# Chunked attention feeding a routed expert layer: SP's flag read and the early group's place moved

## The chip, the cores and the metric

The kernel runs on one core of a Trainium2 chip. A core has TensorE (PE: products, and PEld: the loads of their weights), VectorE (DVE), ScalarE (ACT), GpSimd (POOL) and SyncE (SP, which only issues DMAs here). Every engine takes its instructions strictly in program order and waits on semaphores. The metric is the time of one execution in device microseconds; lower is better.

## The reference

```python
def _attn_ref(q, k, v):                  # q, k, v: 8 x 8 x 576 x 64
    ...
    scores = scale * np.matmul(q_c, k_c.transpose(0, 1, 2, 4, 3))   # within chunks of 64
    scores = scores - np.max(scores, axis=-1, keepdims=True)
    attn = np.exp(scores)
    attn = attn / (np.sum(attn, axis=-1, keepdims=True) + 1e-09)
    out = np.matmul(attn, v_c)
...
def _moe_ref(x, w_gate, w1, w2, capacity):   # x: 4608 x 512, E = 8, F = 1024, capacity 80
    logits = x @ w_gate
    expert_idx = np.argmax(logits, axis=1)
    ...
    gate_w = probs[np.arange(N), expert_idx]
    out = np.zeros((N, D), dtype=np.float32)
    for e in range(E):
        tok_idx = np.where(expert_idx == e)[0]
        ...
        if len(tok_idx) > capacity:      # the 80 tokens of the largest gate weight stay
            gw = gate_w[tok_idx]
            tok_idx = tok_idx[np.argpartition(-gw, capacity)[:capacity]]
        h = np.maximum(x[tok_idx] @ w1[e], 0.0)
        out[tok_idx] = gate_w[tok_idx, None] * (h @ w2[e])
```

The attention's output, as 4608 rows of 512, is the expert layer's x. Rows that no expert keeps are zero.

## The kernel before

**Attention.** 18 pairs of row tiles (36 tiles of 128 rows) run through a pipeline written out by hand: scores, row maxima, exponential, values, division (`divide`), a transpose for the gate (`xtrans`), gate products (`gate_mm`). SP loads q, k, v and stores the rows to a scratch tensor `xs` (`store`). Eight groups of four tiles hold rows 0 to 511 of the eight batches, the ninth (`T == 8`) the last 64 rows of all of them, the "tail". In passing, SP also loads the weights of experts 0 and 1 in 512 KB pieces (`early_pieces`).

**Routing.** For each tile the gate's chain (maximum, exponential, winner, gate weight as a level) runs over DVE, ACT and POOL. Counting products (`tally`) find each expert's threshold; then every kept token gets a place, one-hot matrices (`hot`) and 36 products sum the candidates (`cand`), ranks follow, and `place` yields the row numbers of six groups of 128 expert rows (`gi`), gate weights and targets. `keep_warm(n)` issues n products whose result nobody reads. A flag (`flag_i`) says whether a general path has to run behind the program.

**The early group.** Up to 64 tokens each of experts 0 and 1 from the first 28 tiles are chosen ahead (`spec_...`): two one-hot products for each tile (one for each expert), a sum into row numbers `gi0`, and a gather of 128 rows into `x0`. `spec_units` queues its two layers as 19 units (transposes `turned`, eight `l1`, eight `l2`), and `fill(k)` puts the next k of them on TensorE between steps of the routing. Its buffers `xT0`, `hs0` and `ht0` take turns in the ring of buffers named xT.

**Expert stage.** `experts` takes groups 1 to 5: a gather by POOL (`rows`, tiles xgc), a transpose (xpc), layer 1 in two halves (hc), a transpose (hpc), layer 2 (yc), a multiplication by the gate weight and a scatter to `out`. `LATER` is the order in which SP issues the loads of experts 2 to 7 (`part`: 2 MB each, w1 and w2 apart) and the zeroing of `out` (`clear`: 1 MB each) around these groups. Group 1 needs experts 0 to 2, group 2 experts 2 and 3, group 3 experts 4 and 5, group 4 5 and 6, group 5 6 and 7. The expert stage's memory lies over that of the attention's buffers, so a load also waits for the last reader of what lay there.

## Time and profile before

| | us |
|---|---|
| median of 3 runs | 255.55 (255.5 to 257.46) |
| the profiled execution, its own time | 257.42 |
| its span, first to last instruction | 255.6 |
| PE busy | 226.1 (88%) |
| DVE busy | 118.6 (46%) |
| ACT busy | 67.7 (27%) |
| POOL busy | 57.1 (22%) |

Busy shares are means over stages with different limits, so a stage is read by its windows, its timeline and its waits. Two lines of the page cut the span into 40 slices of 6.39 us each; the one on the DMA engines gives their busy share in tenths:

```
DMA  7999999999999999999400599999999999997211
```

### The profile page before, as it was taken

What the parts mean: (1) busy time and instruction counts of PE and PEld (TensorE: products, weight loads), DVE (VectorE), ACT (ScalarE), POOL (GpSimd) and SP (SyncE); (2) the same over time, 40 slices, a digit from 0 to 9 for tenths busy, and PEclk for the clock granted to TensorE, in tenths of its full rate; (3) what the DMA queues carried; (4) which work ended last, traced back from release to release, by engine and by line L of the source; (5) the groups of instructions that cost most, each with busy time, mean ns of one, the idle gap of its engine ahead of it and who ended that gap; (6) DMA issues with size and microseconds to landing.
All of it is one profiled execution on the core that took longest, in us unless ns stands there. A gap on an engine that the chain in (4) does not pass through costs nothing.

```text
span 255.6 us, 7393 instructions
## 1 busy us (share of the span) xinstructions
PE 226.1 (88%) x3211; PEld 142.1 (56%) x3211; DVE 118.6 (46%) x269; ACT 67.7 (27%) x119; POOL 57.1 (22%) x158
## 2 busy tenths in 40 slices
PE   8699999999999999999999924999809999999980
PEld 5598897888898898888663301233202424232420
DVE  7767696868696878884747210012100211111210
ACT  2214343635363635544051100111000202010000
POOL 9202202222222222385730043000000000000711
PEclk9999999999999999999599995799956999999996
DMA  7999999999999999999400599999999999997211
GB/s 248 393 404 380 383 410 408 407 403 401 393 374 365 408 349 332 374 411 401 164 0 3 171 374 398 398 399 390 407 410 410 406 391 400 398 404 278 106 74 38
DMA packets 34742, 84.73 MB, mean 332 GB/s; under 512 B 3022, under 2 KB 3150, under 8 KB 34704
## 3 DMA queue, kind: packets, MB, share of 16 engines
q1 hardware_dynamic: 33744, 81.31, 83.5%
q0 software_dynamic: 960, 2.88, 3.0%
q8 instruction: 27, 0.44, 0.7%
q14 instruction: 11, 0.09, 0.1%
HBM read 64.00 MB, written 20.45 MB: 330 GB/s over the span
## 4 chain that ended last, share of the span: by engine, by line
PE 69%; SPq 12%; DMA 10%; issue 3%; DVE 2%; ACT 1%; POOL 0%; POOLq 0%; ACTq 0%
PE o L436 14%; PE s L379 12%; PE yc L246 9%; PE hc L213 9%; SPq L1144 8%; DMA w<-in_w 7%; PE px L408 4%; SPq L807 4%; PE pt L408 4%; PE small L491 4%; DMA qb<-in_qk 3%; PE hpc L231 2%; PE hw L776 2%; PE pwarm L776 1%; PE xw L746 1%
## 5 line engine op out<-in xcount | busy, mean ns | idle before, releaser
L213 PE MATMUL hc<-w,xtc 128*32 128x512 f32 x288 | 35.9, 630 | 7.5 <-DMA w<-in_w 7.5
L436 PE MATMUL o<-vb,pT 128*64 128x130 f32 x576 | 36.2, 276 | 0.5 <-ACT pT L417 0.5
L379 PE MATMUL s<-qb 128*64 128x128 f32 x512 | 31.9, 276 | 2.6 <-DMA qb<-in_qk 2.0
L436 PEld LDWEIGHTS o<-vb,pT 128*64 128x64 f32 x576 | 31.7, 135 | 1.7 <-ACT pT L417 0.6
L379 PEld LDWEIGHTS s<-qb 128*64 128x64 f32 x512 | 27.9, 137 | 5.0 <-issue 3.6
L390 DVE TENSOR_REDUCE mx<-s 128x16 f32<-128x1024 f32 x18 | 22.0, 1225 | 14.1 <-PE s L379 13.2
L246 PE MATMUL yc<-w,htc 128*32 128x512 f32 x256 | 28.2, 593 | 0.0
L417 ACT ACTIVATE pT<-pt 128x1024 f32<-128x1024 f32 x18 | 18.3, 1025 | 30.5 <-PE pt L408 28.9
L213 PEld LDWEIGHTS hc<-w,xtc 128*32 128x32 f32 x288 | 9.3, 115 | 29.8 <-issue 21.4
L482 ACT COPY xT<-px 128x1024 f32<-128x1024 f32 x17 | 17.1, 1009 | 23.2 <-PE px L408 23.2
L451 DVE TENSOR_TENSOR x<-o,rc 128x1024 f32<-128x1024 f32 (+1 forms) x20 | 22.4, 1118 | 0.7
L395 DVE TENSOR_TENSOR sm<-s,mx 128x1024 f32<-128x1024 f32 x18 | 22.1, 1228 | 0.6
L265 POOL DMA_INDIRECT out<-x,to x1 | 1.0, 1046 | 81.3 <-SPq L1160 81.3
L246 PEld LDWEIGHTS yc<-w,htc 128*32 128x32 f32 x256 | 8.2, 110 | 18.7 <-issue 18.7
L220 DVE TENSOR_SCALAR hsc<-hc 128x512 f32<-128x512 f32 x5 | 3.5, 692 | 32.1 <-PE hc L213 32.1
L218 ACT ACTIVATE hsc<-hc 128x512 f32<-128x512 f32 x4 | 2.4, 598 | 57.3 <-PE hc L213 57.3
L235 DVE COPY htc<-hpc 128x512 f32<-128x512 f32 x5 | 3.5, 692 | 29.2 <-PE hpc L231 29.2
L592 ACT ACTIVATE lv<-io_b,bo 128x256 bf16<-128x256 bf16 x29 | 12.5, 497 | 3.9 <-DVE bo L572 2.6
L251 DVE TENSOR_SCALAR ysc<-yc,gatec 128x512 f32<-128x512 f32 x4 | 3.0, 750 | 21.2 <-PE yc L246 21.2
L408 PE MATMUL px<-ct,x 64*128 64x64 f32 x272 | 12.4, 229 | 0.5 <-issue 0.5
L408 PE MATMUL pt<-ct,sm 64*128 64x64 f32 x288 | 12.8, 229 | 0.0
L408 PEld LDWEIGHTS pt<-ct,sm 64*128 64x128 f32 x288 | 10.3, 139 | 2.9 <-issue 2.8
(208 smaller groups left out, 268.0 us busy)
## 6 DMA issues: line engine op xcount, KB each, us to landing
w<-in_w SPq DMA_DIRECT2D x12, 2048.0 KB, 20.8
qb<-in_qk SPq DMA_DIRECT2D x32, 512.0 KB, 7.6
vb<-in_vv SPq DMA_DIRECT2D x36, 260.0 KB, 6.8
out<-zero SPq DMA_DIRECT2D x9, 1024.0 KB, 15.4
xs<-x SPq DMA_DIRECT2D x16, 512.0 KB, 7.2
w<-in_w SPq DMA_DIRECT2D x16, 512.0 KB, 7.9
w<-in_qk SPq DMA_DIRECT2D x4, 512.0 KB, 5.2
xs<-x SPq DMA_DIRECT2D x4, 256.0 KB, 8.4
```

Source lines behind the costliest of these rows:

```text
L213: nc.tensor.matmul(h[o:o + 32, :], lhsT=xT[r][:, b, o:o + 32], rhs=getw(groups[r][g])[0][:, b, 512 * f:512 * f + 512], start=(b == 0), sto ...
L246: nc.tensor.matmul(y[o:o + 32, :], lhsT=hT[r][c // 4][:, c % 4, o:o + 32], rhs=getw(groups[r][g])[1][:, c, :], start=(c == 0), stop=(c == ...
L379: nc.tensor.matmul(ps[64 * u:64 * u + 64, t, P * pr:P * pr + P].rearrange("p (h k) -> p h k", h=2), lhsT=t8[:, 1, pr, u, :], rhs=t8[:, 0:3 ...
L390: nc.vector.tensor_reduce(d['mx'], d['s8'], axis=AX.X, op=ALU.max)
L395: nc.vector.tensor_tensor(d['sm'].rearrange("p c k h -> p h c k"), d['s8'], d['mx'][:, :, :, None].to_broadcast([P, 2, 8, 64]), op=ALU.sub ...
L408: nc.tensor.transpose(at[:, 64 * c:64 * c + 64], src(c)[rows], ident[rows, rows])
L417: nc.scalar.activation(d['pT'], pt, AF.Exp, scale=0.125)
L436: nc.tensor.matmul(po[64 * u:64 * u + 64, o:o + 130].rearrange("p (h x) -> p h x", h=2), lhsT=d['pT'][:, u, c:c + 64], rhs=v[:, :, pr, u, ...
L451: nc.vector.tensor_tensor(TT[T][:, r:r + nt, :].rearrange("p r (k h e) -> p (r k) h e", k=4, h=2), pov[..., 0:64], rc[:, :, :, None].to_br ...
L482: nc.scalar.copy(XT[n].rearrange("p c u j -> p u c j"), pm.rearrange("p u (c j) -> p u c j", j=64))
L592: nc.scalar.activation(lv, io_b, AF.Sign, bias=bo[:, rt:rt + 1], scale=-1.0)
L1144: nc.sync.dma_start(w[l], src[e].rearrange("(c p) f -> p c f", p=P))
```

## The change

1. The flag is read by SP behind all loads of the expert stage, no longer ahead of them (`general`, read inside the hand-written part).
2. The early group's `hs0` and `ht0` move into the ring place of `qb2`, and `xT0` into that of `pT`; the one-hot matrices of `hot` leave `qb2` for the places of `x` and `pT`. So other weights lie over them, and the gathers' buffers no longer do.
3. `LATER` puts both first clears ahead of w1 of expert 4, and w2 of expert 4 behind w1 of expert 5.
4. The tail becomes tile group 0 and is stored first; the early group's rows then all lie in the first 3456 rows of `xs`, and tile 3 (rows behind that bound) is left out of it.
5. One product for each early tile yields both experts' row numbers in two columns; the gather becomes two of 64 rows. The products and the gather move ahead of the last tile's gate.
6. Steps of the levels 24 to 27 move from POOL to ACT (`signs`), the count of own tokens covers 28 tiles and moves back, 22 of the 24 keep-warm products behind `spec_gather` go, and the early group's units begin five steps earlier.

```diff
 LG = NT - 1
 HOT = 12
 OB = 171
-LATER = [[(2, 1), (3, 0), (3, 1), (4, 0), (4, 1), (0, 2), (1, 2)], [(5, 0), (6, 0)], [(7, 0), (2, 2), (5, 1), (6, 1)],
-         [(3, 2), (7, 1)] + [(n, 2) for n in range(4, NT)], [], [], []]
+LATER = [[(2, 1), (3, 0), (3, 1), (0, 2), (1, 2), (4, 0)], [(5, 0), (4, 1), (6, 0)],
+         [(7, 0), (2, 2), (5, 1), (6, 1)], [(3, 2), (7, 1)] + [(n, 2) for n in range(4, NT)], [], [], []]
 SPEC = 28
 S0 = 64
+SHOT = ((0, 10), (10, 9), (19, 9))
 
 EARLY = {8: [0], 11: [1], 14: [2], 15: [3, 4], 16: [5, 6, 7, 8], 17: [9, 10, 11], 18: [12], 19: [13, 14], 20: [15]}
 
...
 
-    def rows(t, at):
+    def rows(t, at, n=NT * 512):
 
         return nc.gpsimd.indirect_dma_start(
-            out=t, out_offset=None, in_=xs[:, :],
+            out=t, out_offset=None, in_=xs[0:n, :],
             in_offset=bass.IndirectOffsetOnAxis(ap=at, axis=0),
-            bounds_check=NT * 512 - 1, oob_is_err=False)
+            bounds_check=n - 1, oob_is_err=False)
 
     def experts(pool, pp, gi, si, gate, getw, tag, extra=None, ys0=None):
         groups = [[(4 * r + g) // 3 for g in range(4)] for r in range(NR)]
...
             T, r = divmod(2 * n + 1, 4)
-            if T == 8:
+            if T == 0:
                 for u in range(2):
-                    i = nc.sync.dma_start(
+                    nc.sync.dma_start(
                         xs.rearrange("(b s) d -> s b d", s=576)[
                             512:576, 2 * r - 2 + u:2 * r + 2:2, :],
                         TT[T][64 * u:64 * u + 64, r - 1:r + 1, :])
-                    tc.add_to_no_dep_group("first", i.ins)
             else:
-                i = nc.sync.dma_start(
-                    xs[T * 576:T * 576 + 512].rearrange("(c p) d -> p c d", p=P)[:, r - 1:r + 1],
+                nc.sync.dma_start(
+                    xs[T * 576 - 576:T * 576 - 64].rearrange("(c p) d -> p c d", p=P)[:, r - 1:r + 1],
                     TT[T][:, r - 1:r + 1])
-                if 4 * T >= SPEC:
-                    tc.add_to_no_dep_group("first", i.ins)
 
         def xtrans(n, tag="tp"):
             T, r = divmod(2 * n, 4)
...
                 if 'hot' not in S:
-                    S['hot'] = wk.tile([P, 3, P, HOT], BF16, name="pk", tag="qb2", bufs=1), deque(range(3))
-                oh = S['hot'][0][:, S['hot'][1].popleft()]
+                    pk = wk.tile([P, 2, P, HOT], BF16, name="pk", tag="x")
+                    pl = wk.tile([P, P, HOT], BF16, name="pl", tag="pT")
+                    S['hot'] = deque((pk[:, 0], pk[:, 1], pl))
+                oh = S['hot'].popleft()
                 nc.vector.tensor_tensor(
                     oh[:, :, 0:n], S['io_h'][:, :, 0:n],
                     S['ptok_b'][:, None, rt:rt + n].to_broadcast([P, P, n]), op=ALU.is_equal)
...
+            thr0 = S['thr0'] = gk.tile([P, 2], BF16, name="thr0", tag="thr0", bufs=1)
             with nc.allow_low_precision(reason="whole numbers up to 256"):
                 nc.vector.tensor_scalar(thr0, pn0, 1.0, None, op0=ALU.max)
+
+        def spec_mask():
+            thr0 = S['thr0']
             m0 = S['m0'] = gk.tile([P, 2, SPEC], BF16, name="m0", tag="m0", bufs=1)
             nc.vector.tensor_tensor(m0, kb[:, 0:2, 0:SPEC],
                                     thr0[:, :, None].to_broadcast([P, 2, SPEC]), op=ALU.is_ge)
+            nc.vector.memset(m0[:, :, 3:4], 0.0)
             inc0 = S['inc0'] = gk.tile([P, 2, SPEC], BF16, name="inc0", tag="inc0", bufs=1)
...
 
+        def spec_own():
+            cnt = S['cnt'] = gk.tile([P, NE], BF16, name="cnt", tag="cnt", bufs=1)
+            with nc.allow_low_precision(reason="whole numbers up to 28"):
+                nc.vector.tensor_reduce(cnt, mine[:, 0:SPEC, :].rearrange("p r e -> p e r"),
+                                        axis=AX.X, op=ALU.add)
+
...
             oh = S['oh0', r0]
-            cand0 = S['warm'][0]
+            if 'cand0' not in S:
+                S['cand0'] = ps1.tile([P, 2, 512], F32, name="xw0", tag="tp")[:, 0]
+            cand0 = S['cand0'][0:S0, 0:12].rearrange("p (k e) -> p k e", e=2)
             k = 2 * S.setdefault('chunk0', 0)
             S['chunk0'] += 1
             for j in range(n):
                 rt = r0 + j
-                for e in range(2):
-                    nc.tensor.matmul(
-                        cand0[S0 * e:S0 * e + S0, k:k + 2], lhsT=oh[:, :, j], rhs=comp[:, rt, 0:2, e],
-                        start=j == 0, stop=j == n - 1, tile_position=(0, S0 * e))
+                nc.tensor.matmul(
+                    cand0[:, k:k + 2, :],
+                    lhsT=oh[:, :, j], rhs=comp[:, rt, 0:2, 0:2], start=j == 0, stop=j == n - 1)
 
         def spec_gather():
-            gi0 = mp.tile([P, 1], I32, name="gi0")
+            gi0 = mp.tile([P, 2], I32, name="gi0")
             with nc.allow_low_precision(reason="row numbers are whole and far below 2^24"):
-                nc.vector.tensor_reduce(gi0, S['warm'][0][:, 0:6], axis=AX.X, op=ALU.add)
+                nc.vector.tensor_reduce(
+                    gi0[0:S0], S['cand0'][0:S0, 0:12].rearrange("p (k e) -> p e k", e=2),
+                    axis=AX.X, op=ALU.add)
             x0 = S['x0'] = mp.tile([P, DM], F32, name="x0")
-            apart(rows(x0, gi0), "first")
+            for e in range(2):
+                rows(x0[S0 * e:S0 * e + S0], gi0[0:S0, e:e + 1], 6 * 576)
 
         units = deque()
 
         def spec_units():
-            xT = wk.tile([P, 4, P], F32, name="xT0", tag="xT", bufs=3)
-            hs = wk.tile([P, FF], F32, name="hs0", tag="xT", bufs=3)
-            hT2 = wk.tile([P, 2, 4, P], F32, name="ht0", tag="xT", bufs=3)
-            hT = [hT2[:, f] for f in range(2)]
+            xT = wk.tile([P, 2, 512], F32, name="xT0", tag="pT")[:, 0].rearrange("p (b k) -> p b k", k=P)
+            big = wk.tile([P, 2, FF], F32, name="hs0", tag="qb2", bufs=1)
+            hs = big[:, 0]
+            hT = [big[:, 1, 512 * f:512 * f + 512].rearrange("p (b k) -> p b k", k=P)
+                  for f in range(2)]
             A, B, C = S['warm']
             A4 = A.rearrange("p (b k) -> p b k", k=P)
 
...
             left_add(20)
-            for j in range(24, 28):
-                steps_(nc.gpsimd, j)
+            spec_pos()
             values(35, "s")
-            spec_pos()
+            spec_slot()
+            for r0, n in SHOT:
+                spec_hot(r0, n)
+            xtrans(16)
             gate_mm(7)
             gate_copy(7)
+            for j in range(24, 28):
+                signs(j)
+            for r0, n in SHOT:
+                spec_cand(r0, n)
             divide(34)
-            xtrans(16)
+            spec_gather()
             divide(35)
             store(17)
             early_pieces(20)
-            spec_slot()
             gate_sum(7, gates)
             pops(2)
-            spec_hot(0, 10)
+            spec_own()
             xtrans(17, ("o", "s"))
             gate_mm(8)
-            spec_hot(10, 9)
             flush(gates)
             gate_copy(8)
+            rest(28, "level", "sum")
             psx.close()
             ps1 = psx.enter_context(tc.tile_pool(name="ps2", bufs=1, space=PSUM, reuse_waits="tile"))
             small = S['small'] = ps1.tile([P, 2, 256], F32, name="small2", tag="g")
             two = ps1.tile([P, 2, 512], F32, name="two", tag="s")
             S['warm'] = [ps1.tile([P, 512], F32, name=("xw", "hw", "pwarm")[j], tag=f"o{j}") for j in range(3)]
-            spec_hot(19, 9)
+            spec_units()
             signs(28)
             signs(29)
             gate_sum(8, gates)
             tally(24, 4)
-            spec_cand(0, 10)
-            spec_cand(10, 9)
-            spec_cand(19, 9)
+            fill(1)
             pops(2)
             signs(30)
             signs(31)
             left_add(24)
-            spec_gather()
             flush(gates)
+            rest(32, "sum")
             signs(32)
             for j in range(33, 36):
                 steps_(nc.vector, j)
+            fill(1)
             tally(28, 4)
             left_add(28)
             spec_keep()
-            keep_warm(7)
+            fill(1)
             tally(32, 4)
-            rest(28, "level", "sum")
-            rest(32, "sum")
+            fill(1)
+            threshold()
             rest(32, "inverse", "key")
-            keep_warm(4)
-            threshold()
-            spec_units()
-            keep_warm(6)
+            fill(1)
             mask = gk.tile([P, NE, RT], BF16, name="mask", tag="mask", bufs=1)
             nc.vector.tensor_tensor(
                 mask, kb,
...
             for i, (a, b) in enumerate(((tr_b, mask), (idp, mask), (ones_b, inc))):
                 nc.tensor.matmul(pos.rearrange(fl), lhsT=a, rhs=b.rearrange(fl),
                                  start=i == 0, stop=i == 2)
-            fill(1)
-            keep_warm(5)
-            fill(1)
+            fill(2)
             ptok = S['ptok'] = gk.tile([P, RT], F32, name="ptok", tag="ptok", bufs=1)
             ptok_b = S['ptok_b'] = gk.tile([P, RT], BF16, name="ptok_b", tag="ptok_b", bufs=1)
             with nc.allow_low_precision(reason="whole numbers up to 256"):
...
 
+            homes = {}
             part(2, 0)
             experts(ep, pp, lambda r: (places[0][1][:, r:r + 1] if r < 2 else
                                        places[1][1][:, r - 2:r - 1]),
                     si, gate, weights.get, "c", ahead, S['x0'])
-
-
-    with tc.If(nc.values_load(flag_i[0:1, 0:1], min_val=0, max_val=1) > 0):
+            general = nc.values_load(flag_i[0:1, 0:1], min_val=0, max_val=1)
+
+
+    with tc.If(general > 0):
         with ExitStack() as gctx:
             gp = gctx.enter_context(tc.tile_pool(name="gen", bufs=1))
             lo = gp.tile([P, NE], F32, name="glo")
...
     p = i[:, None]
-    row = np.where(rt < 32, rt // 4 * 576 + rt % 4 * 128 + p,
-                   (2 * (rt - 32) + p // 64) * 576 + 512 + p % 64)
+    row = np.where(rt >= 4, (rt // 4 - 1) * 576 + rt % 4 * 128 + p,
+                   (2 * rt + p // 64) * 576 + 512 + p % 64)
     c[:, C_A:C_A + RT] = row // 64 * 64
     c[:, C_B:C_B + RT] = row % 64
     c[:, C_W8:C_W8 + NE] = NE - np.arange(NE)
...
     t = a[:, :, 512:].reshape(b, h // 2, 2, 64, d).transpose(1, 2, 0, 3, 4)[None]
-    return np.concatenate([m, t], 0).reshape(NT, h // 2, 2, 4, 2, 64, d)
+    return np.concatenate([t, m], 0).reshape(NT, h // 2, 2, 4, 2, 64, d)
 
```

What the order of the built program shows. SP first: before, at the end of the attention (w2_1 is the last early piece, xs the scratch rows, w1_2 to w2_4 the loads of experts 2 to 4, out_0 a clear):

```order
L818 DMA w2_1_1956<-in_w2 128x2x512
L1160 TENSOR_LOAD flag_i_86
L1160 ISA x2
L1144 DMA w1_2_2821<-in_w1 128x4x1024
L1144 DMA w2_2_2823<-in_w2 128x8x512
L1144 DMA w1_3_2825<-in_w1 128x4x1024
L1144 DMA w2_3_2827<-in_w2 128x8x512
L1144 DMA w1_4_2829<-in_w1 128x4x1024
L1144 DMA w2_4_2831<-in_w2 128x8x512
L807 DMA out_0<-zero_75 512x1x512 x2
```

The same place now:

```order
L827 DMA w2_1_1958<-in_w2 128x2x512
L1155 DMA w1_2_2776<-in_w1 128x4x1024
L1155 DMA w2_2_2778<-in_w2 128x8x512
L1155 DMA w1_3_2780<-in_w1 128x4x1024
L1155 DMA w2_3_2782<-in_w2 128x8x512
L816 DMA out_0<-zero_75 512x1x512 x2
L1155 DMA w1_4_2786<-in_w1 128x4x1024
L1155 DMA w1_5_2861<-in_w1 128x4x1024
L1155 DMA w2_4_2863<-in_w2 128x8x512
L1155 DMA w1_6_2865<-in_w1 128x4x1024
L1155 DMA w1_7_2958<-in_w1 128x4x1024
```

and the flag's read, further on:

```order
L1155 DMA w2_6_2963<-in_w2 128x8x512
L816 DMA out_0<-zero_75 512x1x512
L1155 DMA w2_7_3059<-in_w2 128x8x512
L816 DMA out_0<-zero_75 512x1x512 x5
L1170 TENSOR_LOAD flag_i_86
L1170 ISA x2
L1173 COMPARE_AND_BRANCH
```

The read has moved behind the last load and the last clears; two clears stand ahead of w1_4, and w2_4 behind w1_5.

ACT, in the gate of the last tile (lv are level masks of the tiles, ex32 the exponential of the last tile, xT0 the copy of the early group's transposed rows). Before:

```order
L592 ACTIVATE lv28_2353<-io_b_66,bo_79 128x256
L592 ACTIVATE lv29_2355<-io_b_66,bo_79 128x256
L529 ACTIVATE ex32_2359<-sh32_2358 128x32
L592 ACTIVATE lv30_2437<-io_b_66,bo_79 128x256
L592 ACTIVATE lv31_2439<-io_b_66,bo_79 128x256
L592 ACTIVATE lv32_2456<-io_b_66,bo_79 128x256
L770 COPY xT0_2524<-xw_2349 128x512
```

Now:

```order
L590 ACTIVATE lv28_2396<-io_b_66,bo_79 128x256
L590 ACTIVATE lv29_2398<-io_b_66,bo_79 128x256
L779 COPY xT0_2394<-xw_2391 128x512
L527 ACTIVATE ex32_2402<-sh32_2401 128x32
L590 ACTIVATE lv30_2429<-io_b_66,bo_79 128x256
L590 ACTIVATE lv31_2431<-io_b_66,bo_79 128x256
L590 ACTIVATE lv32_2443<-io_b_66,bo_79 128x256
L789 ACTIVATE hs0_2395<-hw_2392 128x512
```

The copy xT0 stood behind all level masks and now stands ahead of the last tile's exponential; the first activation of the early group's layer 1 (hs0) has moved ahead of the routing's ptok.

DVE, from the division of tile 34 (rc34, x8) to the copy of the last transposed tile (xT17; pm0, ptc and pk0 are the early group's places and one-hot matrices, gi0 its row numbers). Before:

```order
L449 TENSOR_SCALAR rc34_2244<-o34_2173 128x8
L450 RECIPROCAL rc34_2244<-rc34_2244 128x8
L451 TENSOR_TENSOR x8_2131<-o34_2173,rc34_2244 128x512
L449 TENSOR_SCALAR rc35_2267<-o35_2214 128x8
L450 RECIPROCAL rc35_2267<-rc35_2267 128x8
L451 TENSOR_TENSOR x8_2131<-o35_2214,rc35_2267 128x512
L718 TENSOR_TENSOR pm0_2274<-small_99,m0_2192 128x56
L720 TENSOR_TENSOR ptc_2275<-pm0_2274 128x28
L561 TENSOR_REDUCE gm28_2283<-small_99 128x4
L528 TENSOR_TENSOR sh28_2279<-small_99,gm28_2283 128x32
L733 TENSOR_TENSOR pk0_2293<-io_h_430,ptc_2275 128x640
L478 COPY xT17_2313<-px17s_2296 128x512
```

Now, from the second and third one-hot group on (pm0, ptc and the first group stand ahead of these rows):

```order
L737 TENSOR_TENSOR pk0_2222<-io_h_432,ptc_2219 128x64x9 x2
L450 TENSOR_SCALAR rc34_2300<-o34_2175 128x8
L451 RECIPROCAL rc34_2300<-rc34_2300 128x8
L452 TENSOR_TENSOR x8_2131<-o34_2175,rc34_2300 128x512
L758 TENSOR_REDUCE gi0_2304<-xw0_2271 64x2
L450 TENSOR_SCALAR rc35_2313<-o35_2209 128x8
L451 RECIPROCAL rc35_2313<-rc35_2313 128x8
L452 TENSOR_TENSOR x8_2131<-o35_2209,rc35_2313 128x512
L559 TENSOR_REDUCE gm28_2324<-small_99 128x4
L526 TENSOR_TENSOR sh28_2320<-small_99,gm28_2324 128x32
L724 TENSOR_REDUCE cnt_2334<-mine_78 128x8
L476 COPY xT17_2354<-px17s_2337 128x512
```

The one-hot groups stand ahead of both divisions, the sum gi0 between them, and the count cnt ahead of the copy.

## Rows read from the trace of the kernel before

**Rows 1.** Waits of SP, which issues the loads: us, times, longest us.

```profile
SPq L1160 <- DVE flag_i L1117: 22.8, 1, 22.8
```

**Rows 2.** Timeline of SP: start us, us, engine, line, operation, out<-in, count.

```profile
117.77 0.86 SPq L818 DMA_DIRECT2D w<-in_w  x1
142.31 21.83 SPq L1144 DMA_DIRECT2D w<-in_w  x6
```

**Rows 3.** Windows: stretch, us, PE PEld DVE ACT POOL, granted clock, DMA share, GB/s.

```profile
124.00:130.00 6.00, 5.58 (x42) 3.63 (x41) 4.91 (x13) 1.37 (x5) 3.52 (x11) 0.64 0.16 51
130.00:136.00 6.00, 6.00 (x76) 3.58 (x76) 2.69 (x15) 2.22 (x9) 1.46 (x2) 1.00 0.01 3
158.00:165.00 7.00, 6.82 (x44) 1.90 (x48) 0.00 (x0) 1.05 (x3) 0.00 (x0) 0.68 1.02 399
165.00:183.00 18.00, 18.00 (x172) 6.15 (x167) 2.08 (x3) 1.89 (x4) 0.00 (x0) 1.00 1.04 396
```

**Rows 4.** Timeline of the expert stage, idle time before and its releaser in brackets.

```profile
149.28 1.10 POOL L177 DMA_INDIRECT xgc<-xs,gic  x1 [17.82 <-PE hw L785]
...
156.39 1.12 PE L202 MATMUL xpc<-ct,xgc 128*128 128x128 f32 x4 [7.92 <-DMA xgc<-xs,gic]
...
158.19 5.74 PE L213 MATMUL hfirst<-w,xtc 128*32 128x512 f32 x32 [0.68 <-ACT xtc L203]
...
191.78 6.00 PE L213 MATMUL hc<-w,xtc 128*32 128x512 f32 x26 [7.51 <-DMA w<-in_w]
```

**Rows 5.** Chain that ended last, by time: start us, us, engine, tile, line.

```profile
124.64 0.87 PE pwarm L669 x4
...
127.64 0.85 PE xw L769 x4
...
129.21 1.06 PE hw L776 x8
130.27 2.09 PE two L1027 x36
...
199.23 3.57 PE hc L213 x32
202.80 6.87 PE yc L246 x64
...
213.10 1.02 PE hpc L231 x8
214.13 0.44 PE xpc L202 x4
```

**Rows 6.** Timeline of the routing.

```profile
113.18 0.69 DVE L451 TENSOR_TENSOR x<-o,rc 128x512 f32<-128x512 f32 x1
...
115.04 0.48 DVE L733 TENSOR_TENSOR pk<-io_h,ptc 128x640 bf16<-128x640 bf16 x1
...
121.57 0.17 DVE L753 TENSOR_REDUCE gi<-xw 128x1 int32<-128x6 f32 x1 [2.78 <-PE xw L746]
...
122.03 1.30 POOL L177 DMA_INDIRECT x<-xs,gi  x1 [3.15 <-DMA xs<-x]
...
123.00 0.29 DVE L572 TENSOR_SCALAR bo<-bb 128x4 f32<-128x4 bf16 x1
...
128.57 0.59 ACT L770 COPY xT<-xw 128x512 f32<-128x512 f32 x1 [4.67 <-PE xw L769]
...
137.55 0.16 DVE L156 TENSOR_REDUCE gic<-small 128x2 int32<-128x4 f32 x1 [1.02 <-PE small L152]
```

**Rows 7.** DMA issues: KB each where known, median us from issue to landing.

```profile
w<-in_w SPq DMA_DIRECT2D x12, 2048.0 KB, 20.8
...
xgc<-xs,gic POOLq DMA_INDIRECT x5, 7.1
...
x<-xs,gi POOLq DMA_INDIRECT x1, 4.0
```

**Rows 8.** Timeline of the end.

```profile
247.99 0.75 DVE L251 TENSOR_SCALAR ysc<-yc,gatec 128x512 f32<-128x512 f32 x1 [6.12 <-PE yc L246]
```

More of the change, by code (lines that the diff above doesn't have):

```diff
@@ L93, in apart @@
         tc.declare_no_dep(
-            inst.ins, group=group, reason="rows of their own",
+            inst.ins, group=group, reason="every store writes rows of its own",
             query=mybir.DependencyQuery(
@@ L617, in tally @@
             U['ph', rt] = ph
-        def own_counts():
-            cnt = S['cnt'] = gk.tile([P, NE], BF16, name="cnt", tag="cnt", bufs=1)
-            with nc.allow_low_precision(reason="whole numbers up to 24"):
-                nc.vector.tensor_reduce(cnt, mine[:, 0:24, :].rearrange("p r e -> p e r"),
-                                        axis=AX.X, op=ALU.add)
         def left_add(rt):
@@ L694, in spec_level, with spec_threshold @@
                 nc.tensor.matmul(pn0, lhsT=ones_b, rhs=S['ge0'][:, b, :], start=b == 0, stop=b == 1)
-        def spec_mask():
-            thr0 = gk.tile([P, 2], BF16, name="thr0", tag="thr0", bufs=1)
+        def spec_threshold():
+            thr0 = S['thr0'] = gk.tile([P, 2], BF16, name="thr0", tag="thr0", bufs=1)
             with nc.allow_low_precision(reason="whole numbers up to 256"):
                 nc.vector.tensor_scalar(thr0, pn0, 1.0, None, op0=ALU.max)
+        def spec_mask():
+            thr0 = S['thr0']
             m0 = S['m0'] = gk.tile([P, 2, SPEC], BF16, name="m0", tag="m0", bufs=1)
@@ L925, in attention_moe @@
                     spec_count()
-                if n == NPAIR - 2:
-                    own_counts()
                 if n < NPAIR - 2:
@@ L936, in attention_moe @@
             xtrans(15)
+            spec_threshold()
             divide(32)
@@ L1134, in attention_moe, with home, part @@
                                                  reuse_waits="tile"))
-            def part(e, l, after=None):
-                w = weights.setdefault(e, [None, None])
-                pool = wp if e in (5, 6) else wp2
-                a, src, n = ((4, w1, FF), (8, w2, DM))[l]
-                w[l] = pool.tile([P, a, n], F32, name=f"w{l + 1}_{e}", tag=f"w{l + 1}")
-                if after is not None:
-                    nc.vector.tensor_copy(w[l][:, 0, 0:1], after)
-                nc.sync.dma_start(w[l], src[e].rearrange("(c p) f -> p c f", p=P))
+            def home(e, l):
+                pool = wp if e in (5, 6) else wp2
+                a, n = ((4, FF), (8, DM))[l]
+                return pool.tile([P, a, n], F32, name=f"w{l + 1}_{e}", tag=f"w{l + 1}")
+            def part(e, l):
+                w = weights.setdefault(e, [None, None])
+                w[l] = homes.pop((e, l), None)
+                if w[l] is None:
+                    w[l] = home(e, l)
+                nc.sync.dma_start(w[l], (w1, w2)[l][e].rearrange("(c p) f -> p c f", p=P))
             def ahead(r):
```

## The prediction, made before the changed kernel was run

> **What bounds the kernel now.** I begin with the waits of SP, since that queue issues every load. It stands 22.8 us at one instruction, the read of the flag [rows 1]. The timeline of SP shows what is queued behind it: the last early piece goes out at 117.77, the first load of experts 2 to 4 at 142.31 [rows 2]. The windows give the price twice. From 130 to 136 the DMA engines are busy 0.01 of the time; from 158 to 183, when the loads come all at once, they move 396 to 399 GB/s without a break [rows 3]. The bill is paid where the loads are used: the timeline of the expert stage shows PE standing 7.51 us for a load ahead of group 3's layer 1 [rows 4].
>
> The second limit is the start of that stage. POOL issues the first gather at 149.28, after 17.82 us without work, released by the last product of the early group's layer (L785), because the gather's buffer lies on that group's buffers; its row numbers (gic) were there at 137.71 [rows 4, 6]. The rows reach PE at 156.39 [rows 4]. The third is the clock: PE's granted clock is 0.64 in the window 124 to 130 and 0.68 in 158 to 165, 1.00 in the others [rows 3], so the first 32 products there take 5.74 us where later ones take 3.57 [rows 4, 5]. Between the two waits lies the routing, a chain from the last tile's gate over the 36 products to gic [rows 5, 6].
>
> **The change part by part.** I follow the path: the end of the last tile's gate (bo, 123.29 [rows 6]), the end of the candidates' products (130.27 + 2.09 = 132.36 [rows 5]), PE's first transposed row of group 1 (156.39), the last layer's end, the end.
>
> *The early group's rows, moved ahead of the gate.* First what it costs DVE. The three one-hot groups (0.48 each [rows 6], 1.4 in all), the two steps ahead of them, the sum (0.17) and the count (bounded by 0.17 and 0.48, two neighbours [rows 6]) now stand ahead of the last copy that the gate needs, and DVE may wait for the 28 products; the 56 of before held it 2.78 [rows 6], so half is 1.4. That is up to 3.9 us; the 2.78 that it stood later go away. Left are 1.1 us at most, and 0 if the products run while DVE divides.
>
> Something longer stands behind it. On PE the transposes of x0 (turned) now stand right after the tally of tile 24, and on ACT the copy xT0 stands ahead of the exponential of the last tile. So the gate's end now waits for x0 to land. When? The one-hot groups began at 115.04, behind both divisions (0.69 and two small steps each, some 1.1), and now begin ahead of them: some 112.6; plus 1.4 and at most 1.4 for the products is 115.4, and the gate products of tiles 28 to 31 stand ahead of those on PE, for which I allow another 1.4: 116.8. The two gathers are issued one after the other, each 1.30 as the one of before [rows 6]: the second at 118.1 to 118.4. A gather landed 4.0 us after issue for x0 and 7.1 in the expert stage, with loads queued [rows 7]; now a load (w1_2) is issued right ahead, so I take the end near 7.1: 125.4, and 122.3 as the other end. Behind that come the transposes 0.85 [rows 5], the copy 0.59 [rows 6], the exponential and the sums to bo, some 1.5 (bo ends 1.7 after gi begins, in the row of before): 3.0 together. The gate ends at 125.3 to 128.5 and not at 123.29: **+2.0 to +5.2**.
>
> From there to the candidates' end it was 9.1 us. 22 keep-warm products (0.87 for 4, so 4.8 us [rows 5]) go and six units of 1.06 [rows 5] come in their place; DVE's chain sets this stretch rather than PE, so I put it at nothing, to +1.0 if the units stand ahead of what routing waits for. The candidates' end moves by +2 to +6; I take **+5**: 137.4.
>
> *The buffers.* From the candidates' end to PE's first row of group 1 it was 156.39 − 132.36 = 24.0. With the gather's buffer free of the early group, what is left is the chain to gic, 137.71 − 132.36 = 5.35 [rows 5, 6], and the gather, 7.1 (156.39 − 149.28 [rows 4]; median 7.1 [rows 7]): 12.5. The units that are left for PE after the candidates (13 of 19, at about 0.9, an estimate from the 0.85 and 1.06) fit into these 12.5 and keep it busy. First row: 137.4 + 12.5 = **149.9**, 6.5 earlier.
>
> *One rule of the Trainium skill speaks against the gathers' new places.* A gather's issue took 1.30 at 122.03, beside DVE's gate, and 1.10 at 149.28, when the routing was over [rows 4, 6], so a neighbour on DVE costs 0.2. The page "SBUF — State Buffer", section "SBUF: two separate sides", says that DVE and GpSimd share a port pair as an exclusive lock, and that GpSimd cannot write the descriptors of its DMAs while DVE runs an operation in a two-port mode. By the row the first gather of group 1 costs 0.2 more beside the ranks; by the rule it could stand for some of DVE's steps one after the other, an estimate of 1.2 for five steps of 0.25. Neither changes the sum beyond its range.
>
> *Flag and loads.* SP no longer stands before the loads. w1_2 goes out near 119 instead of 142.31, w2_2 and w1_3 when the attention's buffers are free, w2_3 and the first clears after the candidates' products, w1_4 after the early group's last product, w1_5 after group 1's second half of layer 1. 2 MB at 396 GB/s [rows 3] is 5.3 us, so the loads of groups 1 and 2 are in by the time that group 1 begins. The narrowest is w1_5, for group 3: issued 8.7 after group 1's first row (1.3 + 3.5 + 3.5 and a little), landed 5.3 + 4.0 later (its bytes, and a latency as the shorter gather's): 18.0. Group 3's layer 1 begins behind layer 1 of groups 1 and 2 and layer 2 of group 1: 1.3 + 4 × 3.5 + 6.87 + 1.02 + 2 × 0.44 = 24.1 by the prices below. The slack is 6 us, so the 7.51 go, and nothing is late next.
>
> *The expert stage then.* Lead 1.3 (transpose and copy: 156.39 to 158.19 was 1.8 with PE at 0.68), ten halves of layer 1 at 3.5 (3.57), five layers 2 at 6.87, five transposes at 1.02, four at 0.44 [rows 5]: 1.3 + 35.0 + 34.35 + 5.1 + 1.76 = **77.5**. Before, it was 247.99 [rows 8] − 156.39 = 91.6; the 14.1 less are the 7.51, the 2.2 of the first products (5.74 − 3.57), and the rest of the same kind: the 26 products behind the hole at 6.00 instead of 2.9 [rows 4], and small things. The tail, 255.6 − 247.99 = 7.6, stays.
>
> *Costed at nothing.* The flag's read stands behind the loads and is over while PE works; were it not covered, it would be one small read behind the last scatter. The tail's stores move to the front, with four issues of 64 rows each for the tail as before, in a stretch that PE fills. The levels' steps go from POOL to ACT in the same stretch. A single product per tile does what two did: 28 fewer, counted above.
>
> **Sum.** 149.9 + 77.5 + 7.6 = 235.0 of span, against 255.6. The profiled execution took 257.42, 1.8 more than its span, so one like it would take 236.8; the median of the runs, 255.55, stands where the span stands. I predict **235.0**, 20.6 less: 6.5 from the stage's start, 14.1 within it.
>
> **The rivals.** *The loads still bind (243).* A load took 20.8 from issue to landing [rows 7], but six were queued together. Were w1_5 to take that, it lands 29.5 after the first row, 5.4 after it is needed, and the clock falls with PE idle, some 2.5 as in the row of 6.00 instead of 2.9: +8. Against it: only few loads are open at a time now. Chance 0.08. *The clock stays low through the routing (247).* In the window 124 to 130 PE's granted clock is 0.64 of 2.4 GHz, part of it at 1.2 [rows 3]; with the keep-warm products gone it could stay at 1.2 until group 1. Of the 24.5 us from the gate's end to group 1's first row, half comes on top at most: +12. Against it: the units are PE work of their own. Chance 0.05. *The change doesn't free the loads (249).* If SP still stands until the routing's end because of buffers, only the gather's 6.5 is won: 255.6 − 6.5. The order of SP and the places of the buffers speak against it. Chance 0.03. *Slower (261).* The gathers queue behind loads issued before them: three loads, 3 × 5.3 = 15.9, hold x0 until 13.7 later than I take, and w2_3 with two clears holds group 1's gather, 7.5 later; PE idles in both and twice starts again at half clock, 2.3 each: 13.7 + 7.5 + 4.6 = 25.8, so 235 + 25.8 = 261. It is slower from 20.6 on, when the two gathers together land that much later. Against it: with six loads queued since 142.31, group 1's gathers still landed in 7.1 [rows 2, 7]. Chance 0.03. *Better than forecast (230).* x0 lands after 4.0, the gate waits for nothing: 3 to 5 less. Chance 0.02.
>
> **How the numbers follow.** The forecast has 0.79, with its own range 232.7 (x0 lands after 4.0, −2.3) to 238 (+1 from the units ahead of the routing, +2 for a part of the clock lost). To leave out no more than 2 in 10 the range reaches into the first rival: 231.0 to 240.5. About 1% of 255.55, 2.6 us, is what a measurement of this kernel can tell from no change. Faster by over 1% is every case but the last slow one and a mix near nothing: 0.95; within 1% 0.02; slower 0.03.
>
> **What would show it.** Right: SP's waits without the flag; w1_2 issued near 119; no stretch of idle DMA after 124; group 1's gather issued near 143 and PE's transposes of it near 150; no hole ahead of group 3. A wait of ACT's copy xT0 and of PE ahead of the transposes of x0, some 3 to 6 us long, would show the step that costs. Wrong: a gather of x0 that lands over 8 us after issue, a granted clock of about 0.5 in the window of the candidates' products, or PE waiting for a load in group 2 or 3.

## The result: faster, and less so than forecast

Median 241.81 us (240.48 to 242.49, 4 runs) against 256.09 (255.5 to 257.46) beside it: ratio 0.943, 95% interval 0.937 to 0.949. The forecast was 235.0 with a range up to 240.5; the sign was right and the time missed the range by 1.3 us. The profiled execution took 242.49 with a span of 240.6.

Where the load queue stood shows first. SP's waits in the changed kernel (us in total, times, longest us) have the flag no more [rows 1]; SP now stands at loads whose place is still in use:

```profile
SPq L1155 <- PE hc L214: 18.5, 3, 8.8
...
SPq L1155 <- DVE pk L643: 11.3, 1, 11.3
SPq L1155 <- PE hw L794: 10.5, 1, 10.5
```

and SP's timeline has the first load of the expert stage at 120.33, where it was at 142.31 [rows 2]:

```profile
119.77 0.47 SPq L827 DMA_DIRECT2D w<-in_w  x1
120.33 21.93 SPq L1155 DMA_DIRECT2D w<-in_w  x4
142.36 1.66 SPq L816 DMA_DIRECT2D out<-zero  x2
154.55 18.00 SPq L1155 DMA_DIRECT2D w<-in_w  x5
```

The windows of the changed kernel (columns as in [rows 3]):

```profile
118.00:124.00 6.00, 4.95 (x53) 3.83 (x54) 3.10 (x12) 1.49 (x5) 3.58 (x8) 0.52 1.01 340
124.00:130.00 6.00, 2.15 (x19) 1.20 (x21) 1.34 (x9) 1.73 (x6) 0.22 (x1) 0.50 1.03 348
130.00:136.00 6.00, 6.00 (x58) 1.77 (x54) 1.91 (x10) 0.69 (x2) 0.00 (x0) 0.56 1.04 388
136.00:142.00 6.00, 5.39 (x60) 2.60 (x60) 4.33 (x8) 3.34 (x10) 5.34 (x10) 1.00 0.90 358
160.00:183.00 23.00, 23.00 (x211) 7.92 (x210) 2.82 (x4) 2.91 (x6) 0.00 (x0) 1.00 1.02 386
```

The idle stretch of the DMA engines is gone (0.01 in 130 to 136 [rows 3], now 1.04), and from 160 on PE is busy without a hole. But in 124 to 130 PE works 2.15 of 6 us, and from 118 to 136 its granted clock is 0.50 to 0.56, the lower level of 1.2 GHz. The chain that ended last, in that part (start us, us, engine, tile, line):

```profile
114.79 3.31 PE xw L751 x28
118.13 0.16 DVE gi L758
...
120.12 7.29 DMA x<-xs,gi
127.41 0.14 issue
127.55 1.10 PE xw L778 x4
128.67 0.59 ACT xT L779
129.31 1.94 PE hw L785 x8
...
154.40 0.86 PE xpc L203 x4
```

The early group's rows are now on the path: 28 products, the gather (7.29), the transposes, the copy, a unit of layer 1 at half clock. ACT's timeline shows the last tile's exponential (ex) right behind that copy, for which ACT stood 4.27 us, and the timelines of the other engines give the gate's end (bo), two more units of the early group's layer 1, the end of the candidates' products (two), group 1's gather, its layer 1 and the last output step:

```profile
128.67 0.59 ACT L779 COPY xT<-xw 128x512 f32<-128x512 f32 x1 [4.27 <-PE xw L778]
129.15 0.23 ACT L527 ACTIVATE ex<-sh 128x32 f32<-128x32 f32 x1
...
130.25 0.17 DVE L570 TENSOR_SCALAR bo<-bb 128x4 f32<-128x4 bf16 x1
...
132.12 1.94 PE L785 MATMUL hw<-w,xT 128*32 128x512 f32 x8
...
134.35 1.49 PE L785 MATMUL hw<-w,xT 128*32 128x512 f32 x8
...
142.12 0.22 PE L1034 MATMUL two<-comp,pk 128*128 128x48 bf16 x2
...
148.04 1.12 POOL L178 DMA_INDIRECT xgc<-xs,gic  x1 [5.98 <-DVE bt L1056]
...
155.92 3.64 PE L214 MATMUL hfirst<-w,xtc 128*32 128x512 f32 x32 [0.87 <-ACT xtc L204]
...
232.70 0.75 DVE L252 TENSOR_SCALAR ysc<-yc,gatec 128x512 f32<-128x512 f32 x1 [6.12 <-PE yc L247]
```

Group 1's first row is on PE at 154.40 (156.39 before [rows 4]), the stage from there to the last output step takes 78.3 us (91.6 before), the end 7.9.

### The profile page after: what moved, and what is told of

Read it like the earlier page. It is cut to its first block, busy times and chain, and to the rows that moved or that the text cites. A ratio compares the mean times of both kernels' runs of the same rounds, so it can differ in the third digit from the quotient of the medians.

```text
span 240.6 us, 7297 instructions
## 1 busy us (share of the span) xinstructions
PE 220.5 (92%) x3161; PEld 139.0 (58%) x3161; DVE 118.5 (49%) x270; ACT 69.4 (29%) x123; POOL 54.3 (23%) x155
## 4 chain that ended last, share of the span: by engine, by line
PE 78%; DMA 10%; issue 3%; ACT 2%; SPq 2%; DVE 2%; POOL 1%; POOLq 0%
PE hc L214 13%; PE o L437 12%; PE s L380 12%; PE yc L247 11%; PE px L409 4%; PE pt L409 4%; DMA qb<-in_qk 4%; DMA w<-in_w 3%; DMA x<-xs,gi 3%; PE hw L794 3%; PE yfirst L247 3%; PE small L489 3%; PE hw L785 2%; PE hpc L232 2%; PE hfirst L214 2%
## 5 line engine op out<-in xcount | busy, mean ns | idle before, releaser
L214 PE MATMUL hc<-w,xtc 128*32 128x512 f32 x288 | 32.5, 594 | 0.0
L214 PEld LDWEIGHTS hc<-w,xtc 128*32 128x32 f32 x288 | 8.8, 110 | 19.4 <-issue 19.4
L590 ACT ACTIVATE lv<-io_b,bo 128x256 bf16<-128x256 bf16 x33 | 14.2, 498 | 0.3 <-DVE bo L570 0.3
```

Of the source, the lines that this page charges most:

```text
L214: nc.tensor.matmul(h[o:o + 32, :], lhsT=xT[r][:, b, o:o + 32], rhs=getw(groups[r][g])[0][:, b, 512 * f:512 * f + 512], start=(b == 0), sto ...
L590: nc.scalar.activation(lv, io_b, AF.Sign, bias=bo[:, rt:rt + 1], scale=-1.0)
```

## The experiments

Ten runs. Each time is a median beside runs of the kernel before on the same chip; ratios are to those, with their intervals. One execution of a kernel differs from the next by up to 1.9%, much of it ahead of the routing: the changed kernel, run again unaltered, had every mark some 2 us earlier. So the marks of the routing are compared from the start of the early group's one-hot groups in the same trace (112.48 in the changed kernel).

**1 and 2: the flag alone, and all but the flag.** The kernel before with the flag's read moved:

```diff
                     si, gate, weights.get, "c", ahead, S['x0'])
+            general = nc.values_load(flag_i[0:1, 0:1], min_val=0, max_val=1)
-    with tc.If(nc.values_load(flag_i[0:1, 0:1], min_val=0, max_val=1) > 0):
+    with tc.If(general > 0):
```

> The kernel before with one edit: SP reads the flag behind all loads and clears. Theory (the flag's read is where the gain came from, the moved buffers and the earlier gather gave little): the hole of 7.51 us ahead of group 3 and most of the half-clock products go, group 1 starts where it did, near 156: 240 to 244 us. Rival (the loads also need the early group's buffers to be out of their way, or the gathers suffer behind the loads): SP stands at a load instead of at the flag until about 149, and 250 to 256 us result.

And the changed kernel with the read put back:

```diff
             homes = {}
+            general = nc.values_load(flag_i[0:1, 0:1], min_val=0, max_val=1)
             part(2, 0)
...
-            general = nc.values_load(flag_i[0:1, 0:1], min_val=0, max_val=1)
```

> The changed kernel with one edit taken back: SP reads the flag ahead of all loads of the expert stage. Theory: the flag is ready near 150, so the first load goes out some 30 us later than in the changed kernel, PE waits for weights in groups 1 to 3, and 248 to 256 us result; and with no load queued beside it the second gather of x0 lands 4 to 5 us after its issue, not 7.4, so the last tile's gate ends near 128 and not at 130.4. Rival (the early group's place gives the gain): 241 to 245 us; or the gather lands after 7 us here too, and then the loads are not what made it slow.

The flag alone: 245.92 us, ratio 0.965 (0.955 to 0.974), somewhat above the expected 240 to 244. Everything but the flag: 261.38 us, 1.023 (1.015 to 1.032): slower than the kernel before, and above the expected 248 to 256. So the four corners are about 255 to 256 (neither), 246 (flag), 261 (the rest), 242 (both). In the trace of the flag alone, PE still waits for group 1's rows as before, group 3's hole is gone, and the one early gather, the same instruction as before, lands after 7.0 us where it landed after 4.0 [rows 7]:

```profile
156.46 1.11 PE L202 MATMUL xpc<-ct,xgc 128*128 128x128 f32 x4 [7.50 <-DMA xgc<-xs,gic]
158.25 4.91 PE L213 MATMUL hfirst<-w,xtc 128*32 128x512 f32 x32 [0.67 <-ACT xtc L203]
...
119.72 23.20 SPq L1144 DMA_DIRECT2D w<-in_w  x6
...
x<-xs,gi POOLq DMA_INDIRECT x1, 7.0
```

From PE's first row (156.46) to the last output step (236.30) it is 79.8 us. So 11.8 of the stage's 13.3 us are the flag's; the other 1.5 and the start's 2 came with the other edits. Counted from its own one-hot groups, group 1's row comes 1.9 us later than in the kernel before (43.3 us against 41.4): the slower gather costs some of what the flag gains. With the flag back, SP stands 29.7 us for it and the first load goes out at 150.69, since the flag itself comes later; PE then waits for the rows, and for weights twice:

```profile
SPq L1166 <- DVE flag_i L1124: 29.7, 1, 29.7
```

```profile
158.19 1.12 PE L203 MATMUL xpc<-ct,xgc 128*128 128x128 f32 x4 [5.49 <-DMA xgc<-xs,gic]
159.98 5.69 PE L214 MATMUL hfirst<-w,xtc 128*32 128x512 f32 x32 [0.67 <-ACT xtc L204]
...
173.94 5.25 PE L214 MATMUL hc<-w,xtc 128*32 128x512 f32 x30 [3.27 <-DMA w<-in_w]
...
194.57 5.17 PE L214 MATMUL hc<-w,xtc 128*32 128x512 f32 x26 [2.63 <-DMA w<-in_w]
```

Part of my expectation fell: with no load of the expert stage in the queue, x0's second gather was on PE 6.3 us after its issue (120.00 to 126.32), not 4 to 5, with an early piece issued at 119.64 just ahead of it. Experiment 1 shows a load beside a gather making it slower, but here the loads of the expert stage account for only 1 us of it, by one trace each.

**3: the early group's first unit behind the last tile's gate.**

```diff
             tally(24, 4)
-            fill(1)
             pops(2)
...
-            fill(1)
             tally(28, 4)
             left_add(28)
             spec_keep()
-            fill(1)
+            fill(2)
```

> The changed kernel with the early group's first unit (transposes of x0 and the copy xT0) put on its engines behind the count of tile 28's group, no longer ahead of the last tile's exponential. Theory (the last tile's gate waits for x0's rows through ACT's order): the gate ends near 126 to 127 and not at 130.4, the candidates' products 2.5 to 4 us earlier, 237 to 239 us. Rival (the clock is the cause and the wait hides behind it): under 1 us, 240.5 to 242 us, with the gate's end moved but the units and transposes in the way later.

239.71 us, 0.939 (0.931 to 0.947), between the theory's 237 to 239 and the rival's 240.5 to 242. The gate ends 13.7 us after the one-hot groups' start and not 17.9, so the wait through ACT's order is real. But the stretch behind it grows from 11.9 to 14.1: DVE now stands for the last tally, which PE has queued behind the transposes and a unit at half clock:

```profile
129.85 0.17 DVE L627 SCALAR_TENSOR_TENSOR ge<-small,left 128x16 bf16<-128x16 f32 x1 [3.85 <-PE small L612]
```

Of 4.2 us, 1.7 arrive at group 1's layer 1: the wait moved one step on.

**4 and 5: unread products where PE stood.** Ahead of the transposes of x0 (`tally(24, 4)`, then `fill(1)`), first 11 of them, then 24 and 5 behind:

```diff
             tally(24, 4)
+            keep_warm(11)
             fill(1)
             pops(2)
```

> The changed kernel with 11 products that nobody reads put on PE between the tally of tile 24 and the transposes of x0, where PE stood 3.2 us. Theory (the low clock behind that wait lengthens the four units that stand in the routing's way, 1.94 instead of 1.06 each): the granted clock in 130 to 136 rises from 0.56 to over 0.8, the units take 1.06, the candidates' products end some 2 us earlier, 238.5 to 240 us. Rival (DVE's chain sets that stretch): the units get shorter and the end stays, 240.5 to 242.5 us.

```diff
             tally(24, 4)
+            keep_warm(24)
             fill(1)
+            keep_warm(5)
             pops(2)
```

> The run with 11 unread products again, with 24 of them ahead of the transposes of x0 and 5 behind, so that PE hardly stands before the early group's first unit. Theory (the low clock there costs the routing some 2 us): the granted clock in 130 to 136 rises from 0.56 to over 0.9, the first three units take 1.06 and not 1.94, the candidates' products end near 140.3 and not at 142.3, the span is 2 us shorter, 238 to 239. Rival (the clock comes back late whatever PE does, or DVE's chain sets the stretch): the clock stays below 0.7 or the end stays, 240 to 241.

Eleven: 239.24 us, 0.933 (0.923 to 0.943). Its four executions took 241.91 and 240.97 us, with a mean granted clock of 0.966 over the span, and 237.51 and 237.50, with 0.978 and 0.976, which are values of experiment 5 (0.976 to 0.980). The trace is of the 241.91: PE still stood 1.90 us, the first two units took 1.93 and 1.94, the stretch behind the gate 11.8. It shows a filling that did not hold the clock; how the two executions of 237.5 came to theirs is not shown. Twenty-four: 238.18 us, 0.929 (0.921 to 0.936). Windows with eleven:

```profile
124.00:130.00 6.00, 3.42 (x30) 1.99 (x32) 1.44 (x10) 1.93 (x6) 0.22 (x1) 0.78 0.96 336
130.00:136.00 6.00, 6.00 (x58) 1.82 (x54) 2.01 (x11) 0.55 (x2) 0.00 (x0) 0.58 1.04 389
```

and with twenty-four and five, where PE stood 0.41 us and then worked on:

```profile
124.00:130.00 6.00, 5.46 (x61) 3.78 (x57) 2.16 (x14) 2.13 (x6) 0.22 (x1) 1.00 0.99 347
130.00:136.00 6.00, 5.81 (x62) 1.59 (x58) 3.98 (x13) 1.66 (x6) 2.83 (x6) 1.00 1.04 387
```

There the transposes take 0.63 instead of 1.09, the units 1.06 instead of 1.94, and from the gate to the candidates it is 9.5 us instead of 11.9. Group 1's layer 1 begins 3.2 us earlier. The marks of this run:

```profile
129.32 0.17 DVE L570 TENSOR_SCALAR bo<-bb 128x4 f32<-128x4 bf16 x1
...
138.77 0.22 PE L1036 MATMUL two<-comp,pk 128*128 128x48 bf16 x2
```

**6: weights side by side.**

```diff
-S['hot0'] = wk.tile([P, 3, S0, 10], BF16, ...
+S['hot0'] = wk.tile([P, 3, 10, S0], BF16, ...
...
-                oh[:, :, 0:n], S['io_h'][:, 0:S0, 0:n],
-                S['ptc'][:, None, r0:r0 + n].to_broadcast([P, S0, n]), op=ALU.is_equal)
+                oh[:, 0:n, :], io_b[:, None, P:P + S0].to_broadcast([P, n, S0]),
+                S['ptc'][:, r0:r0 + n, None].to_broadcast([P, n, S0]), op=ALU.is_equal)
...
-                    lhsT=oh[:, :, j], rhs=comp[:, rt, 0:2, 0:2], ...
+                    lhsT=oh[:, j, :], rhs=comp[:, rt, 0:2, 0:2], ...
```

> The changed kernel with the early group's one-hot matrices laid out so that the 64 columns of a tile lie side by side, where before a tile's columns lay 10 apart. Theory (each of the 28 products takes 118 ns because its weights are read with that stride): they take 55 to 65 ns, 1.7 us and not 3.3 in all, the gathers go out 1.6 us earlier less what DVE's groups get longer (1.34 to 1.6 or 2), and 239 to 240.5 us result. Rival (a product waits for its own weights and these take that long anyway): 118 ns each again and 241 to 243 us.

238.62 us, 0.930 (0.922 to 0.938), a little below the expected 239 to 240.5. DVE's groups and PE's products, first this run, then the changed kernel:

```profile
112.08 2.17 DVE L737 TENSOR_TENSOR pk<-io_b,ptc 128x640 bf16<-128x640 bf16 x3
...
114.38 1.02 PE L751 MATMUL xw<-comp,pk 128*64 128x4 bf16 x28 [0.18 <-DVE rc L450]
```

```profile
112.48 1.34 DVE L737 TENSOR_TENSOR pk<-io_h,ptc 128x640 bf16<-128x640 bf16 x3
...
114.79 3.30 PE L751 MATMUL xw<-comp,pk 128*64 128x4 bf16 x28 [0.18 <-ACT xT L480]
```

36 ns for a product instead of 118, below the 55 to 65 expected; the groups cost DVE 0.8 more, and the second gather goes out 5.3 us after their start instead of 7.6. Layer 1 of group 1 begins 1.9 earlier.

**7 and 8: no unit ahead of the threshold; and that with the new layout.**

```diff
             tally(24, 4)
-            fill(1)
+            keep_warm(3)
             pops(2)
...
-            fill(1)
             tally(28, 4)
             left_add(28)
             spec_keep()
-            fill(1)
+            keep_warm(7)
             tally(32, 4)
-            fill(1)
+            keep_warm(4)
             threshold()
             rest(32, "inverse", "key")
+            keep_warm(2)
             fill(1)
...
-            fill(2)
+            fill(3)
             ptok = S['ptok'] = gk.tile([P, RT], F32, name="ptok", tag="ptok", bufs=1)
```

> The changed kernel with no unit of the early group ahead of the last tally and the threshold (unread products stand in their places, as in the kernel before), and the transposes of x0 behind them. Theory (units in the routing's way on PE, and the wait for x0, cost the stretch from the gate's end to the candidates' products): the gate ends near 125, the candidates' products end 9 to 10 us later, near 134.5, where they ended at 142.3; then 17 units are left for PE, some 17 us with the routing's products between them, so that group 1's rows are turned near 150 to 151: 237 to 238 us. Rival (what is not done early is only done late): 239 to 241 us, since PE's work is the same and was the bound.

> The two edits before together. Theory: 1 to 1.5 us less than the second alone, 236 to 237 us. Rival: the same as that one, since the early group's rows no longer hold the gate.

239.11 us, 0.933 (0.924 to 0.942), and 235.36 us, 0.916 (0.907 to 0.925). The expectation says "later" of the candidates' end and means earlier, 134.5 against 142.3; it was 134.6. In the first run, the gate ends 13.7 us after the one-hot groups' start and the candidates 8.3 behind it; then it takes 17.5 to group 1's layer 1 instead of 13.6, with PE on the units left over until 149.5. Half of the rival's point holds: 3.9 of 7.8 us are given back, and the time is at the rival's edge (239 to 241). Group 1's transposes began without a wait for the rows, but PE then stood for ACT's copy of them, 1.97 us where it is 0.87 in the changed kernel; why the copy came late is not shown:

```profile
152.07 3.64 PE L214 MATMUL hfirst<-w,xtc 128*32 128x512 f32 x32 [1.97 <-ACT xtc L204]
```

The two together are the fastest version measured, 8% below the kernel before, and 3.7 us below the first alone where 1 to 1.5 were expected, so the rival is out. The trace is of an execution of 237.33 us, where the others took 233.67 to 236.25, and its stretches are not in the table below.

**9 and 10: the changed kernel again, and the new layout with unread products.**

```diff
             tally(24, 4)
+            keep_warm(36)
             fill(1)
+            keep_warm(5)
             pops(2)
```

> The changed kernel itself, unaltered, beside the next one on the same chip: 240.5 to 242.5 us, the gate's end near 130.4 and the candidates' end near 142.3 again.

> The changed kernel with the one-hot columns side by side, and 36 unread products ahead of the transposes of x0 and 5 behind. Theory (the two costs are separate, so they add: 2.5 us by the products, 3.7 by the clock): x0 lands near 125, the candidates' products end near 136.5, 234 to 236 us. Rival (they are one: the 28 slow products were what brought the clock down): no better than either alone, 237 to 239 us.

240.48 us, 0.937 (0.931 to 0.943), and 236.68 us, 0.923 (0.917 to 0.929). In 9 the gate ends at 128.5 and the candidates at 139.9, 2 us ahead of 130.4 and 142.3, as its one-hot groups are. The time of 10 is a little above the 234 to 236 expected and just under the rival's 237 to 239, and its interval overlaps those of experiments 5 and 6. From the one-hot groups' start to group 1's layer 1 it gains 5.9 us on the changed kernel, against 1.9 (new layout) and 3.2 (clock) alone. So by the marks the two costs add; but this is one trace, of an execution of 234.81 us, and the times alone don't show it. In 118 to 136 its granted clock is 1.00 throughout:

```profile
118.00:124.00 6.00, 5.61 (x59) 4.71 (x56) 0.79 (x5) 1.40 (x4) 1.00 (x5) 1.00 1.06 379
124.00:130.00 6.00, 5.87 (x67) 1.93 (x66) 3.72 (x17) 2.08 (x6) 1.17 (x3) 1.00 1.02 397
130.00:136.00 6.00, 5.38 (x64) 3.54 (x62) 3.23 (x6) 3.52 (x11) 4.46 (x9) 1.00 1.04 398
```

The rival, that the slow products brought the clock down, is not put aside by this. In all seven traces with the strided layout (the changed kernel and experiments 2, 3, 4, 5, 7 and 9) the clock fell while the 28 products ran or within 1.5 us of their end. With the weights side by side it did not in 6 and 10, and did in 8 (0.50 from 116 to 119 of its trace).

The stretches, worked out from these traces (from the start of the first one-hot group to bo's end, from there to the last candidates' product, from there to the start of group 1's layer 1):

```
                         gate   candidates   layer 1    sum
forecast                 15.7      9.1         13.8     38.6
the changed kernel       17.9     11.9         13.6     43.4
again                    17.8     11.4         13.9     43.1
3 unit behind the gate   13.7     14.1         13.9     41.7
4 eleven products        17.8     11.8         13.3     42.9
5 24 and 5 products      17.2      9.5         13.6     40.3
6 side by side           15.8     12.0         13.7     41.5
7 gate first             13.7      8.3         17.5     39.6
10 layout and products   14.6      9.5         13.4     37.5
```

## Why the prediction had the gain right and two terms of its price wrong

*Flag and loads: right.* The 22.8 us wait, the idle DMA engines and the hole ahead of group 3 went, and nothing came late next. I had 14.1 us of gain in the stage, it is 13.3 (78.3 us against 77.5). Experiment 1 shows that the flag's edit alone is 9 us of the result; undoing it (experiment 2) shows that the rest of the change without it costs time.

*The buffers: right.* From the candidates' end to group 1's rows I took 12.5; it is 12.06 (154.40 − 142.34), with PE busy on the units up to the rows. No run takes this edit back alone; the row of the gather shows that it no longer waits for the early group (released by the ranks' bt).

*The early rows ahead of the gate: the right path, a term too small.* That the gate would wait for x0 through PE's transposes and ACT's copy is what the chain shows, and the 3.0 from landing to bo measured 2.9. The failed step is "half is 1.4" for the 28 products. They took 3.30, as long as the 56 of before, which went in pairs to the two halves of the columns, 60 ns each: halving the count saved nothing. Experiment 6 cuts them to 1.02 with the same count, by the layout alone, so the stride of the weights set their time; that the two halves of a pair were read side by side in the kernel before is my reading, which no run takes apart. The missing 1.9 is most of the 2.1 by which the gate was late (130.42 against 128.3); the landing, 7.4 instead of 7.1, adds 0.3, and smaller errors nearly cancel (the products began 0.5 earlier than I allowed, the second gather was issued 0.6 later behind them).

*Keep-warm products: costed at nothing, worth 2.4.* From the gate's end to the candidates I put 9.1 "at nothing, to +1.0 if the units stand ahead"; it was 11.9. The failed step is "DVE's chain sets this stretch rather than PE": the units that the change puts in the routing's way set it, by the clock that they ran at. The clock fell in both kernels behind the 28 or 56 narrow products, by the windows of the kernel before (first two lines) and of the changed one (last two):

```profile
118.20:121.50 3.30, 3.30 (x60) 3.28 (x58) 0.46 (x3) 1.82 (x5) 0.52 (x3) 1.00 1.05 404
121.50:124.00 2.50, 2.48 (x27) 1.72 (x26) 2.26 (x12) 0.51 (x1) 1.86 (x3) 0.50 0.72 276
```

```profile
115.00:118.00 3.00, 3.00 (x28) 3.00 (x27) 0.00 (x0) 1.54 (x4) 0.00 (x0) 1.00 1.05 404
118.00:121.00 3.00, 2.30 (x24) 1.77 (x26) 2.37 (x8) 0.80 (x2) 2.10 (x2) 0.53 1.02 374
```

Before, PE then worked on, keep-warm products among it, and the clock was 0.84 in 128 to 129 and 1.00 from 129 on, ahead of the first unit (129.21). Now PE stood for x0, and the clock stayed at 0.50 until 135: the four units ahead of the routing's place products took 1.94, 1.94, 1.49 and 1.06, where they take 1.06 or 1.07 each in experiment 5, which is 2.2 of the 2.8. I had this as a rival, the clock staying at 1.2, at up to 12 us and 0.05, as if it were all or nothing; it belonged in the forecast with its size. (Its 24.5 us count from the landing of x0 that I took, 125.4; from the gate's end, 128.3, it is 21.6.) Experiment 5 gives the stretch back (9.5) with PE kept at work; the one trace of experiment 4, with a shorter filling, doesn't.

*The rest.* The stage's 0.8 and the end's 0.3 are small. The sum of the steps, +2.1 + 2.8 − 0.4 + 0.8 + 0.3, is the 5.6 us by which the span is longer than 235.0. Another 1.2 is that I set the median equal to the span: every execution of this kernel takes about 1.9 us more than its span, and the profiled one of before was that much above its median, the profiled one here only 0.7.

*The port rule.* The Trainium skill, "SBUF — State Buffer", section "SBUF: two separate sides", could have had group 1's gather stand for DVE's steps. By the trace it took 1.12 at 148.04, with the ranks running on DVE beside it, and 1.10 at 149.28 before with DVE done [rows 4]: nothing of the 1.2 shows on POOL, and nothing of the 0.2 that I had put down to a neighbour on DVE. No run isolates a DVE operation in that mode, so this neither refutes the rule nor needs it.

*What stays open.* Why the second gather lands 6.3 to 7.6 us after issue wherever PE waited for it in a version of the changed kernel: the loads of the expert stage make up 1 of it (experiment 2), the early piece and the other gather were not taken apart. And the 2 us by which one execution comes to the routing earlier than the next.

## What to carry to other kernels

When a queue's first wait is for a result that only a rare path needs, put the wait last; but do it with whatever else is moved, since a second edit that pushes that result later (here by 8 us) turns into a loss if the wait stays. When an early result is put ahead of something critical "because it is ready", follow its consumers on each in-order engine: here ACT's copy and PE's transposes waited for a gather with the last tile's gate behind them. And price a group of small products by how their weights lie and not by their number alone, and what takes the place of unread products by the clock that they held.

## What the runs showed of the hardware

- 28 products with 128x64 weights and 4 columns took 3.30 us with the weights' columns 10 elements apart (118 ns each) and 1.02 us with them side by side (36 ns), at a granted clock of 1.00 in both (115 to 118 in the changed kernel, 112 to 115 in experiment 6). In experiment 9 the strided ones took 3.30 too, at 0.50 from 115 on, behind the first two microseconds. 56 of them in the kernel before, in pairs in the two halves of the columns, took 3.3 too, at 1.00 (118.2 to 121.5), with columns 10 apart.
- The same gather instruction landed 4.0 us after issue with no load of the expert stage queued, and 7.0 with one issued 0.5 us ahead (experiment 1, one trace each).
- With PE standing 3.2 us in 124 to 130 the granted clock was 0.50 there and 0.56 in the next six us of unbroken work; with that gap filled (experiment 5) it was 1.00 in both. In the trace of experiment 4 it was 1.00 in 125 to 128, where PE stood 1.90 us, and 0.50 again in 128.6 to 130.
